# A block of linear attention and a gated feed-forward network: where one of three sums of w2 is made, and the order of steps in the key pairs, the query rounds and the reload

## The chip, the cores and the metric

The kernel runs on one core of a Trainium2 chip. The metric is the device time of one execution in microseconds (us). The kernel before takes 1144.45 us, the median of three runs (1141.81 to 1144.91).

## The reference

`x` has 2048 rows (S) and 576 columns (D). There are 32 heads of 18 columns, and the feed-forward network has 4608 columns (F). Everything is float32.

```python
phi = lambda t: where(t > 0, t + 1, exp(t)) + 1e-6
xn  = layernorm(x)
q, k, v = split(xn @ wqkv)                       # 32 heads of 18
kv  = einsum("bhsd,bhse->bhde", phi(k), v);  z = sum over s of phi(k)
o   = einsum("bhqd,bhde->bhqe", phi(q), kv) / (einsum("bhqd,bhd->bhq", phi(q), z) + 1e-6)
s   = o @ wo
g   = silu(gelu(xn @ w1 + b1) @ w2 + b2)
out = x + s * g
```

## The kernel before

**The arithmetic.** TensorE (PE) does every product in a form called fp32r. To keep float32's accuracy an operand is split in two: ScalarE (ACT) casts it to the high part, and VectorE (DVE) subtracts that from the operand to get the low part; a product is then three matmuls (high by high, high by low, low by high). Most of the large products are also cut into two by two blocks and done with seven block products instead of eight. Such products need sums and differences of blocks as operands; they are numbered 1 to 7, and 4, 5 and 6 (of w2; for other tensors others too) work on operands that are differences of blocks. GpSimd (POOL) makes most of these differences, DVE some.

**Key pairs.** The 16 row tiles of x (128 rows each) go two by two through the pairs p = 0 to 7. For a pair, x is normalised (`x_stats` on DVE and POOL, `x_norm` on ACT, line L260, tile xn), transposed on PE (`transpose_x`, L270, into the one transpose bank pt), cast (`x_hi`, xH), copied (`x_raw`, L284, scr), and subtracted (`x_lo`, xL). `x_sum` (L310, scr) makes the differences, `s_hi` and `s_lo` split them into xSH and xSL, and `x_store` writes all four to DRAM (x_dram). PE then makes k with the seven products (class Proj; four banks a, b, z and e; in the order 1, 6, 7, 5, 2, 4, 3; matmuls at L349, with ACT's copy of the first product, m1, at L361, and DVE's u1 and u2 at L357 and L367), v of both tiles plainly (class Plain, L404; ACT copies the result at L411), and adds k and v into the state (`do_state`) one pair later. Banks are handed round, so that product 7 of a pair (bank z) takes the bank that the first copy of v of the pair before has to leave. phi is `phi_exp` (ACT, L435), `phi_max` (DVE, L438) and `phi_add` (ACT, L441).

**What sets the order.** Every pair and every round has 14 steps (NSP). `add(step, fn, ...)` puts a call into the plan, and `at_step(step)` issues what stands there right behind PE's matmuls of that step. A number in these tables thus sets where an operation stands in its engine's queue. PE, DVE, ACT and POOL each keep the order in which the code is written, and each works its queue strictly in that order. The DMAs are issued by SyncE (SP).

**Query rounds.** Rounds r = 0 to 9 do the same for q, a pair of tiles in each: Proj, phi, the denominator (`den_mul` on POOL, `den_sum` on DVE, `den_div` on POOL, which writes p into pbuf), `pad` (ACT, L832), `transpose_p` (bank ptp), `p_hi` and `p_lo` (th, tl), and `Attend`, the product with kw. kw is the state times wo, made once in round 0 (`fold_wo`); its row blocks reach their place through DMAs into the tiles kr, and `split_kw` casts (L774, kw_h) and subtracts (kw_l) each.

**w2's differences.** The chunks of the feed-forward network need three differences of blocks of w2, operands 5, 6 and 4, for each of nine chunks of w2. All 27 are made ahead, in pairs 2 to 6 and rounds 2 to 7: `w2_load` reads the chunk, `w2_sum` (POOL) subtracts, `w2_hi` (ACT, L503) and `w2_lo` (DVE, L509, tile w2o) split, and the split operand is stored in DRAM. `W2_FIRST` and the loop at `2 <= r <= 7` hold the steps.

**Feed-forward chunks.** There are 9 chunks of F, and for each 2 halves of the rows; all chunks of the first half run first. A chunk has 28 steps (NS). Steps 0 to 13 are two Ups (class Up, matmuls at L1123): seven products each in the order 1, 6, 7, 5, 2, 3, 4, with banks a, b, zy, e; behind product 1 ACT copies a to mid (L1140), behind 6 DVE adds b (L1143), behind 7 it adds zy (L1146), behind 5 it writes b from e and mid (L1149), which frees e for product 3; gelu follows on ACT (g, L1131). Steps 14 to 27 are the Down products (bank pm, L1254): seven, each in two parts, in the order 1, 2, 7, 4, 5, 3, 6, and DVE adds each into macc (L1261). The operands of the Down products from gelu's result are sums on POOL (L1213 to L1222) and splits (`HOps`, h_h on ACT at L899, h_l on DVE at L902), at the steps of the table PH. Weights: class W1 loads and splits w1 (the tables P0 and P1; its differences at L918 to L924, tile w1t), class W2 loads a chunk of w2 (w2raw), makes operand 7 (`sum7`, L1176) and splits operands 1, 2, 7 and 3 at the steps of `PW2`. In the first half all split operands are also stored; the second half only loads them (W1Loaded, `W2.load`). Operands 5, 6 and 4 are loaded in the first half too (`W2_SUMS_NEXT`). At the end of the first half's last chunk, `x_swap` (L1396) reloads the four x tensors (xH, xL, xSH, xSL) from x_dram for the second half.

```python
    PW2 = {1: 3, 2: 4, 7: 5, 3: 20}
    W2_SUMS_NEXT = {4: 21, 5: 23, 6: 27}
```

Of the kernel before, what the change touches and what calls it, by code (L numbers as in the profile page):

```python
# [15 lines left out]
P = 128  # L16
# [26 lines left out]
def linear_attention_gated_ffn(ctx, tc, x, wqkv, wo, w1, b1, w2, b2, out):  # L43
# [420 lines left out]
    T_OPS = (5, 6, 4)  # L464
# [24 lines left out]
    def w2_sum(j):  # L489
        c, i = j // 3, T_OPS[j % 3]  # L490
        dst, a, b = w2_block(c, i)
        nc.gpsimd.tensor_tensor(dst, a, b, op=SUB)

    def w2_hi(j):
        if j > 8 and j % 3 == 2:
            halves = [w1p.tile([P, 3 * 2 * P], F32R, tag="wb", name=f"w2o{j}{v}") for v in "hl"]
            w2op[j] = [
                (u[:, : 2 * HD].rearrange("p (a d) -> p a d", a=2), v) for v, u in enumerate(halves)
            ]
        else:  # L500
            t = w1r.tile([P, 2, 2, HD], F32R, tag="stw", name=f"w2o{j}")
            w2op[j] = [(t[:, 0], 0), (t[:, 1], 1), (t, slice(0, 2))]
        nc.scalar.copy(w2op[j][0][0], w2_block(j // 3, T_OPS[j % 3])[0])  # L503

    def w2_lo(j):
        c, i = j // 3, T_OPS[j % 3]
        ops = w2op.pop(j)
        (h, _), (l, _) = ops[:2]
        nc.vector.tensor_tensor(l, w2_block(c, i)[0], h.bitcast(F32), op=SUB)  # L509
        w2_dram[c, i] = d = dram.tile([P, 2, 2, HD], F32, name=f"op_{c}_{i}")  # L510
        for t, v in ops[2:] or ops:
            nc.sync.dma_start(d[:, v], t.bitcast(F32))
# [53 lines left out]
    split_v(4, rest_v, DV)  # L566
    plain_v(0, 0).part(0, N14)
# [11 lines left out]
    x_hi(1, 0), x_lo(1, 0)  # L579
    x_raw(1, 0)  # L580
    x_norm(1, 1)
    s_hi(0), s_lo(0)
    load_x(2, 0)
    load_x(2, 1)
    x_store(0)
    plain_v(0, 1).part(0, N14)
    phi_exp(k_t[1], e_t[1]), phi_max(k_t[1], e_t[1])
    transpose_x(1, 1)
    x_stats(2, 0)
    x_hi(1, 1), x_lo_tmp(1), x_lo(1, 1)  # L590
    phi_add(k_t[1])
# [15 lines left out]
    W2_FIRST = {2: (0, 1), 3: (2, 3), 4: (4, 5), 5: (6, 7), 6: (8,)}  # L607

    def plan_pair(p):
# [19 lines left out]
        if p == 1:  # L629
            sums(1, (0, 0, 0, 1, 1), 2, 3, GP)  # L630
            for s in range(2):
                add(base + 8, k_sum, k_ts[0][s])
# [4 lines left out]
            add(base + 3, x_raw, 2, 0)  # L637
            add(base + 3, x_lo, 2, 0)
            add(base + 5, transpose_x, 2, 1)
            add(base + 5, x_hi, 2, 1)  # L640
            add(base + 6, x_lo, 2, 1)
            sums(2, (6, 6, 6, 6, 7), 8, 9, GP)
            add(base + 6, x_lo_tmp, 2)
            add(base + 7, wkq.split_sums, 1, DV)
            prepare(3, 0, 4, 6, 10, 11)
            prepare(3, 1, 7, 12, None, None)
# [3 lines left out]
            add(base + 5, wkq.split_sums, 0, DV)  # L650
        else:
            if p + 2 < NPAIR:
                prepare(p + 2, 0, 0, 5, 10, 11)
                prepare(p + 2, 1, 7, 11, None, None)
# [3 lines left out]
            if p + 1 < NPAIR:  # L658
                q = p + 1
                add(base + 2, transpose_x, q, 1)  # L660
                add(base + 2, x_hi, q, 1)
                add(base + 4, x_lo, q, 1)
                sums(q, (3, 3, 4, 4, 5), 7, 9, DV)
                add(base + 8, x_lo_tmp, q)
        ka, kb = k_ts[p % 2]
        ea, eb = e_t
        if p == 1:
# [3 lines left out]
            add(base + 9, k_sum, ka)  # L671
# [7 lines left out]
        add(base + 8, phi_add, kb)  # L679
        add(base + 10, k_sum, kb)  # L680
# [297 lines left out]
    for r in range(NPAIR + 2):  # L978
# [6 lines left out]
        if 2 <= r <= NPAIR:  # L985
            add(base, den_mul, r - 1, 1)
            add(base + 2, den_sum, r - 1, 0)
            add(base + 2, den_div, r - 1, 0)
            add(base + 3, den_sum, r - 1, 1)
            add(base + 3, den_div, r - 1, 1)  # L990
        if 1 <= r < NPAIR:
            add(base + 12, den_mul, r, 0)
            add(base + 4, pad, 0)
            add(base + 6, pad, 1)
# [5 lines left out]
        if 1 <= r < NPAIR:  # L1000
            a, b = q_tiles(r)
            add(base + 7, phi_exp, a, e_bufs[0])
            add(base + 7, phi_exp, b, e_bufs[1])
            add(base + 7, phi_max, a, e_bufs[0])
            add(base + 8, phi_max, b, e_bufs[1])
            add(base + 8, phi_add, a)
            add(base + (9 if r > 1 else 8), phi_add, b)
# [558 lines left out]
```

## Time and profile before

| | |
|---|---|
| median of 3 runs | 1144.45 us (1141.81 to 1144.91) |
| the profiled execution | 1145.28 us, span 1143.6 us |
| mean granted clock of TensorE | 0.992 of full speed |
| TensorE busy | 97% of the span |
| VectorE, ScalarE, GpSimd busy | 72%, 44%, 41% |
| DMA | 262 MB, 230 GB/s over the span |
| chain of work that ended last, by engine | PE 78%, DVE 7%, ACT 6%, DMA 5%, issue 2%, POOL 1% |

The profile shows one execution. "Busy" counts an engine's instructions, without the time that it waits; the chain that ended last is followed back from the last instruction, at each step to what released it. The nine chunks of the first half run from about 311 to 720 us, those of the second half from about 720 us to the end; the key pairs run up to about 150 us, and the query rounds behind them. A row of groups or of the timeline gives the start (or the line), the duration, the engine, the line, the operation, the tile written and the tiles read, the shapes, and in brackets the time for which the engine stood idle ahead of it and what ended that.

### The profile page before, as it was taken

The numbers are of one execution on the slowest core, as the hardware profiler recorded it, in microseconds if no ns is written. First come the engines' busy times: TensorE is split into PE (matmuls) and PEld (weight loads), VectorE is DVE, ScalarE is ACT, GpSimd is POOL, SyncE is SP. The second block draws the span as 40 slices with busy tenths as digits, with TensorE's granted clock in tenths as the row PEclk, the third lists the DMA queues.
The fourth block names the chain that finished last, engine by engine and source line by source line (L and its number), as shares of the span: only waits on it lengthen the run. The fifth ranks groups of instructions, "written<-read, shape, count | busy, mean of one in ns | idle before, by whom it ended". The sixth has DMA issues, their size and how long they took to land.

```text
span 1143.6 us, 18714 instructions
## 1 busy us (share of the span) xinstructions
PE 1108.3 (97%) x6924; PEld 1020.3 (89%) x6924; DVE 827.6 (72%) x1250; ACT 503.4 (44%) x913; POOL 473.8 (41%) x403
## 2 busy tenths in 40 slices
PE   8899998999999999999999999899999999999997
PEld 7799996999989989989889899798998998989987
DVE  5877755888687988878879888475574664755766
ACT  6756544544554454444544545333243242332342
POOL 5644342766552544535525543224132332241340
PEclk9999998999999999999999999899999999999999
DMA  5666535697788477495584769977666766667243
GB/s 198 251 231 263 211 108 165 232 321 262 265 307 299 170 267 260 167 333 189 215 319 172 263 242 353 358 277 227 212 203 212 231 196 222 209 206 225 83 140 117
DMA packets 91260, 262.48 MB, mean 230 GB/s; under 512 B 9822, under 2 KB 20574, under 8 KB 89120
## 3 DMA queue, kind: packets, MB, share of 16 engines
q1 hardware_dynamic: 91167, 261.27, 65.1%
q8 instruction: 55, 0.90, 0.3%
q14 instruction: 38, 0.30, 0.1%
HBM read 159.75 MB, written 100.60 MB: 228 GB/s over the span
## 4 chain that ended last, share of the span: by engine, by line
PE 78%; DVE 7%; ACT 6%; DMA 5%; issue 2%; POOL 1%; SPq 0%; DVEq 0%; ACTq 0%; POOLq 0%
PE pm L1254 32%; PE e L1123 12%; PE zy L1123 10%; PE a L1123 10%; PE b L1123 4%; DMA xSL<-x_dram 2%; PE pl L404 2%; PE pd L1371 2%; DVE w2o L509 2%; PE ps_s L872 1%; PE ps_kva L457 1%; PE e L349 1%; PE z L349 1%; DVE k L438 1%; DMA kr<-kw 1%
## 5 line engine op out<-in xcount | busy, mean ns | idle before, releaser
L1261 DVE TENSOR_TENSOR macc<-pm,macc 128x576 f32<-128x576 f32 x218 | 164.3, 754 | 56.8 <-PE pm L1254 56.2
L899 ACT CAST h_h<-g 128x512 fp32r<-128x512 f32 x204 | 120.9, 621 | 139.9 <-PE pm L1254 138.7
L902 DVE TENSOR_TENSOR h_l<-g,h_h 128x512 fp32r<-128x512 f32 x204 | 172.6, 846 | 0.0
L1222 POOL TENSOR_TENSOR mid<-g 128x512 f32<-128x512 f32 x34 | 44.0, 1295 | 197.1 <-ACT g L1131 197.1
L1123 PE MATMUL a<-xH,wa 128*128 128x512 f32 x360 | 117.1, 390 | 0.0
L1123 PEld LDWEIGHTS a<-xH,wa 128*128 128x128 f32 x360 | 67.6, 188 | 13.7
L1131 ACT ACTIVATE g<-b,b1c 128x512 f32<-128x512 f32 x36 | 24.8, 690 | 123.2 <-DVE b L1149 123.2
L1140 ACT COPY mid<-a 128x512 f32<-128x512 f32 x36 | 21.1, 585 | 108.7 <-PE a L1123 108.6
L1123 PE MATMUL e<-xSH,wb 128*128 128x512 f32 x216 | 67.8, 395 | 0.2 <-DVE b L1149 0.2
L1143 DVE TENSOR_TENSOR mid<-b,mid 128x512 f32<-128x512 f32 x36 | 24.8, 690 | 51.3 <-PE b L1123 40.1
L1219 POOL TENSOR_TENSOR g<-g 128x512 f32<-128x512 f32 x34 | 52.5, 1544 | 13.1 <-DVE h_l L902 11.8
L1216 POOL TENSOR_TENSOR g<-g 128x512 f32<-128x512 f32 x34 | 49.5, 1456 | 17.9 <-DVE h_l L902 16.6
L1123 PE MATMUL a<-xL,wa 128*128 128x512 f32 x144 | 56.2, 390 | 0.0
L1342 POOL TENSOR_TENSOR fin1l<-fin1h,fin1l 128x288 f32<-128x288 f32 x8 | 6.4, 805 | 120.0 <-DMA fin1l<-s_dram 78.1
L924 POOL TENSOR_TENSOR w1t<-w1raw 128x256 f32<-128x256 f32 x18 | 16.9, 939 | 84.8 <-DVE w L902 81.2
L1123 PEld LDWEIGHTS e<-xSH,wb 128*128 128x128 f32 x216 | 40.5, 188 | 12.7 <-DVE b L1149 4.5
L1123 PE MATMUL zy<-xSH,w 128*128 128x512 f32 x144 | 51.1, 396 | 0.0
L1123 PE MATMUL b<-xSH,w 128*128 128x512 f32 x144 | 50.9, 394 | 0.0
L1123 PE MATMUL e<-xSH,w 128*128 128x512 f32 x144 | 50.6, 392 | 0.0
L1123 PE MATMUL zy<-xH,w 128*128 128x512 f32 x144 | 50.2, 389 | 0.0
L1213 POOL TENSOR_TENSOR g<-g 128x512 f32<-128x512 f32 x34 | 47.7, 1402 | 2.7
L1156 DVE TENSOR_TENSOR e<-e,mid 128x512 f32<-128x512 f32 x36 | 25.1, 697 | 28.9 <-PE e L1123 28.9
(922 smaller groups left out, 3600.5 us busy)
## 6 DMA issues: line engine op xcount, KB each, us to landing
op<-w SPq DMA_DIRECT2D x72, 256.0 KB
w<-op SPq DMA_DIRECT2D x72, 256.0 KB
op<-w2o SPq DMA_DIRECT2D x21, 576.0 KB
w1raw<-w SPq DMA_DIRECT2D x18, 640.0 KB
w2raw<-w SPq DMA_DIRECT2D x10, 1152.0 KB
op_a<-wa SPq DMA_DIRECT2D x18, 640.0 KB
wa<-op_a SPq DMA_DIRECT2D x18, 640.0 KB
w2r<-w SPq DMA_DIRECT2D x6, 1152.0 KB
```

What stands on the lines that cost most here:

```text
L899: nc.scalar.copy(pair[0], src)
L902: eng.tensor_tensor(pair[1], src, pair[0].bitcast(F32), op=SUB)
L1123: nc.tensor.matmul(ps.rearrange("p (c j) -> p c j", c=4), st, mv, start=first and n == 0, stop=n == len(seq) - 1, skip_group_check=True,)
L1131: nc.scalar.activation(g, ps, AF.Gelu_apprx_tanh, bias=b1c[:, f : f + 1])
L1143: tt(u1_sb, B, m1_sb, op=ADD)
L1156: tt(E, E, u1_sb, op=ADD)
L1213: tt(src[5, pr], A(1, 0), A(1, 1), op=ADD)
L1216: tt(src[6, pr], src[5, pr], A(0, 0), op=SUB)
L1219: tt(src[3, pr], A(0, 1), src[6, pr], op=SUB)
L1222: tt(src[7, pr], A(0, 0), A(1, 0), op=SUB)
L1254: nc.tensor.matmul(ps[:, q, :HD], hs[p][st][:, cs], m[:, p, :], start=(n == 0 and i not in CHAIN), stop=(n == len(seq) - 1), skip_group_ch ...
L1261: nc.vector.tensor_tensor(dst, src, dst, op=ADD)
```

## The change

Four things are changed.

- *w2.* Only operands 5 and 6 (and 4 for chunk 0) are still made ahead, so 19 of the 27 sums stay in the pairs and rounds. Operand 4 of chunks 1 to 8 is made in the feed-forward chunk before: the raw chunk is loaded at step 8 instead of 22, `sum7` goes from step 2 of the chunk to step 20 of the one before, operand 2 is split at step 21, a new `sum4` makes operand 4 in operand 2's place by two subtractions on POOL at step 22, and its split follows at steps 24 and 25. Of `PW2`, operand 7 goes from step 5 to 4 and operand 3 from 20 to 6.
- *Key pairs.* In pair 1 the sums of x go ahead of phi, `x_raw` ahead of `x_lo`. In pairs 2 to 6 the norm of the next pair's second tile moves from step 11 to step 0 of the next pair, its transposes from step 2 to 3, and the sums and `x_lo` behind them; `phi_add` of the second tile goes from step 8 to 10 in all pairs.
- *Query rounds.* In rounds 0 to 2 the splits of kw, the denominators and parts of phi move to later steps.
- *The reload.* The four x tensors are reloaded in the order xSL, xSH, xL, xH at steps 12 and 13, where it was xH, xL at 13 and xSH, xSL at 15; the weight loads of that chunk move to behind them.

```diff
-    T_OPS = (5, 6, 4)
+    SUMS = [(0, 5), (0, 6), (0, 4)] + [(c, i) for c in range(1, NC) for i in (5, 6)]
...
-    x_hi(1, 0), x_lo(1, 0)
+    x_hi(1, 0)
     x_raw(1, 0)
+    x_lo(1, 0)
...
-    phi_exp(k_t[1], e_t[1]), phi_max(k_t[1], e_t[1])
+    phi_exp(k_t[1], e_t[1])
...
-    W2_FIRST = {2: (0, 1), 3: (2, 3), 4: (4, 5), 5: (6, 7), 6: (8,)}
+    W2_FIRST = {2: (0,), 3: (1, 2), 4: (3,), 5: (4, 5), 6: (6,)}
...
         if p == 1:
-            sums(1, (0, 0, 0, 1, 1), 2, 3, GP)
+            sums(1, (0, 0, 0, 1, 1), 1, 5, GP)
+            add(base, phi_max, k_ts[0][1], e_t[1])
+            add(base, phi_add, k_ts[0][1])
...
-                prepare(p + 2, 1, 7, 11, None, None)
+                add(base + 7, x_stats, p + 2, 1)
...
-                add(base + 2, transpose_x, q, 1)
-                add(base + 2, x_hi, q, 1)
-                add(base + 4, x_lo, q, 1)
-                sums(q, (3, 3, 4, 4, 5), 7, 9, DV)
-                add(base + 8, x_lo_tmp, q)
+                add(base, x_norm, q, 1)
+                add(base + 3, transpose_x, q, 1)
+                add(base + 3, x_hi, q, 1)
+                sums(q, (4, 4, 4, 5, 5), 7, 9, DV)
+                add(base + 5, x_lo, q, 1)
+                add(base + 6, x_lo_tmp, q)
...
-        add(base + 8, phi_add, kb)
+        add(base + 10, phi_add, kb)
...
+            late = 2 * (r == 2)
...
+            at = base + 2 * (r == 2)
+            add(at + 7, phi_exp, a, e_bufs[0])
...
-            add(base + 3, split_kw, 2, nc.vector)
-            add(base + 5, split_kw, 3, nc.vector)
+            add(base + 6, split_kw, 2, nc.vector)
+            add(base + 8, split_kw, 3, nc.vector)
...
-            n = 3 * (r + 1)
-            for j in range(3):
-                add(base + (0, 3, 3)[j], w2_sum, n + j)
...
+            n = 2 * r + 3
+            for j in range(2):
+                add(base + ((0, 3) if r > 2 else (4, 5))[j], w2_sum, n + j)
...
             split_kw(0, nc.vector)
-            for s in range(2):
-                den_all(0, s)
-            split_kw(1, nc.vector)
+            den_all(0, 0)
+            add(base + NSP + 2, den_all, 0, 1)
+            add(base + NSP + 3, split_kw, 1, nc.vector)
...
+        def sum4(self):
+            tt = nc.gpsimd.tensor_tensor
+            self.src[4] = self.src[2]
+            tt(self.src[4], self.src[2], self.src[7], op=SUB)
+            tt(self.src[4], self.src[4], self.src[1], op=SUB)
...
-    PW2 = {1: 3, 2: 4, 7: 5, 3: 20}
-    W2_SUMS_NEXT = {4: 21, 5: 23, 6: 27}
+    PW2 = {1: 3, 7: 4, 3: 6}
+    W2_SUMS_NEXT = {5: 23, 6: 27}
...
-            add(base + 22, w2t[step + 1].load_raw)
+            nxt = w2t[step + 1]
+            add(base + 8, nxt.load_raw)
+            add(base + 20, nxt.sum7)
+            add(base + 21, nxt.hi, 2)
+            add(base + 21, nxt.lo, 2)
+            add(base + 22, nxt.sum4)
+            add(base + 24, nxt.hi, 4)
+            add(base + 25, nxt.lo, 4)
...
-                for k, at in ((0, 13), (1, 13), (2, 15), (3, 15)):
+                for k, at in ((2, 12), (3, 12), (1, 13), (0, 13)):
                     add(base + at, x_swap, k)
```

The change takes lines out, so lines of the kernel after are 6 to 8 lower up to about L1160. The instructions of the places that the next part speaks of follow, in the order in which an engine gets them. A row is the line, the operation, the tile written and the tiles read, and the shape; numbers behind a name tell tiles of the same name apart.

ScalarE at the end of key pair 3, before: L441 is `phi_add`, L411 the copies of v, L503 the cast of w2's difference, L278 `x_hi`, L284 `x_raw`, L260 `x_norm`.

```order
L435 ACTIVATE e_161<-k_165,c_85 128x576
L441 ACTIVATE k_165<-k_165,c_86 128x576
L411 COPY v_158<-pl_1046 128x288
L411 COPY v_158<-pl_1047 128x288
L503 CAST w2o_1097<-w2r_718 128x576
L278 CAST xH<-pt_1099 128x640
L284 COPY scr<-pt_1099 128x640
L260 ACTIVATE xn_1126<-x_824,mv_1061 128x576
```

And after:

```order
L435 ACTIVATE e_161<-k_165,c_85 128x576
L411 COPY v_158<-pl_1041 128x288
L411 COPY v_158<-pl_1042 128x288
L496 CAST w2o_1090<-w2r_461 128x576
L278 CAST xH<-pt_1092 128x640
L441 ACTIVATE k_165<-k_165,c_86 128x576
L284 COPY scr<-pt_1092 128x640
L411 COPY v_159<-pl_1104 128x288
L411 COPY v_159<-pl_1105 128x288
L361 COPY mu_153<-a_1145 128x288
L260 ACTIVATE xn_1167<-x_823,mv_1056 128x576
```

The copies of the second v (v_159) and the copy of m1 of the next pair (mu) now stand ahead of the norm of the next pair's second tile.

ScalarE in query rounds 1 and 2, before: L774 is the cast of `split_kw`, L361 the copy of m1, L832 `pad`, L847 `p_hi`, L435 `phi_exp`, L441 `phi_add`.

```order
L774 CAST kw_h<-kw_2041 128x576
L774 CAST kw_h<-kr_2058 128x576
L361 COPY scr<-a_2113 128x288
L774 CAST kw_h<-kr_2071 128x576
L373 ACTIVATE scr<-a_2113,c_84 128x288
L832 COPY pbuf_2036<-pbuf_2036 128x64
L847 CAST th_2176<-ptp_2170 128x640
L774 CAST kw_h<-kr_2080 128x576
L832 COPY pbuf_2037<-pbuf_2037 128x64
L435 ACTIVATE e_2038<-scr,c_85 128x576
L435 ACTIVATE scr<-scr,c_85 128x576
L441 ACTIVATE scr<-scr,c_86 128x576 x2
```

And after:

```order
L361 COPY scr<-a_2094 128x288
L768 CAST kw_h<-kr_2046 128x576
L373 ACTIVATE scr<-a_2094,c_84 128x288
L826 COPY pbuf_2024<-pbuf_2024 128x64
L841 CAST th_2162<-ptp_2156 128x640
L826 COPY pbuf_2025<-pbuf_2025 128x64
L768 CAST kw_h<-kr_2059 128x576
L435 ACTIVATE e_2026<-scr,c_85 128x576
L435 ACTIVATE scr<-scr,c_85 128x576
L768 CAST kw_h<-kr_2068 128x576
L361 COPY scr<-a_2188 128x288
```

Each cast of a kr now stands behind the copy of m1 or the pads that it stood ahead of; the cast of the last kr stands ahead of the copy of m1 of round 2 (a_2188).

VectorE in the second Up of a chunk of the first half, before: L902 is a split (w_3__ of w2, h_l of gelu's result), L1156 and L1160 the ends of products 3 and 4 of the first Up, the other lines as above.

```order
L1156 TENSOR_TENSOR e_5119<-e_5119,mid 128x512
L902 TENSOR_TENSOR w_3__5224<-w2raw_5003,w_3__5224 128x576
L1160 TENSOR_TENSOR zy_5118<-zy_5118,mid 128x512
L1143 TENSOR_TENSOR mid<-b_5241,mid 128x512
L1146 TENSOR_TENSOR mid<-zy_5242,mid 128x512
L902 TENSOR_TENSOR h_l<-g,h_h 128x512
L1149 TENSOR_TENSOR b_5241<-e_5243,mid 128x512
```

And after:

```order
L896 TENSOR_TENSOR w_3__5166<-w2raw_4722,w_3__5166 128x576
L1151 TENSOR_TENSOR e_5080<-e_5080,mid 128x512
L1155 TENSOR_TENSOR zy_5079<-zy_5079,mid 128x512
L896 TENSOR_TENSOR w_3__5195<-w2raw_4722,w_3__5195 128x576
L1138 TENSOR_TENSOR mid<-b_5201,mid 128x512
L1141 TENSOR_TENSOR mid<-zy_5202,mid 128x512
L896 TENSOR_TENSOR h_l<-g,h_h 128x512
L1144 TENSOR_TENSOR b_5201<-e_5203,mid 128x512
```

The last of the w2 splits in this stretch (w_3__5195, operand 3) now stands between zy and mid<-b; before, it was the split of operand 7, ahead of zy.

88 lines of the change are left out of this document (39 added, 49 removed).

## The prediction

> **What bounds the kernel now.** I read the page's first part, then TensorE's waits, then stretches of the span, then rows of single places.
>
> ```profile
> span 1143.6 us, 18714 instructions
> PE 1108.3 (97%) x6924; PEld 1020.3 (89%) x6924; DVE 827.6 (72%) x1250; ACT 503.4 (44%) x913; POOL 473.8 (41%) x403
> ```
>
> TensorE is the bound nearly everywhere. The change neither adds nor removes a matmul (five transposes move by one step), so it can only remove TensorE's stalls or make new ones.
>
> TensorE's waits (who waited, for whom: us in total, times, longest):
>
> ```profile
> PE z L349 <- ACT v L411: 5.0, 5, 1.0
> PE b L1123 <- DMA xSL<-x_dram: 4.4, 1, 4.4
> PE pt L270 <- DVE scr L310: 2.8, 1, 2.8
> PE ptp L840 <- ACT pbuf L832: 2.8, 1, 2.8
> PE a L349 <- ACT scr L361: 2.7, 1, 2.7
> PE z L349 <- DVE scr L367: 2.0, 6, 0.8
> PE e L349 <- DVE rt L357: 1.1, 3, 0.6
> PE pt L270 <- ACT wkq_h L156: 1.1, 1, 1.1
> PE a L349 <- ACT v L411: 0.9, 1, 0.9
> PE e L349 <- DVE scr L357: 0.7, 3, 0.2
> ```
>
> Some 23 us of waits, nearly all at places that the diff touches. None is in the first half of the feed-forward chunks, where the change puts work in.
>
> Stretches (us; busy time of each engine; then granted clock, DMA share, GB/s): key pairs 0 and 1; query rounds 1 and 2; a chunk of the first half; the reload; the first and the second chunk of the second half.
>
> ```profile
> 0.00:55.85 55.85, 45.70 (x311) 42.75 (x312) 40.41 (x85) 37.64 (x66) 33.78 (x46) 0.97 0.61 220
> 162.45:204.37 41.92, 35.02 (x208) 31.04 (x209) 25.53 (x50) 18.23 (x37) 11.68 (x9) 0.92 0.41 136
> 446.96:492.43 45.47, 45.46 (x270) 41.10 (x269) 38.24 (x55) 21.15 (x40) 21.03 (x17) 1.00 0.64 236
> 700.00:724.00 24.00, 21.50 (x157) 20.84 (x155) 20.14 (x26) 10.81 (x15) 8.76 (x6) 1.00 1.02 403
> 719.72:772.29 52.57, 48.22 (x271) 43.13 (x269) 31.44 (x42) 19.20 (x28) 14.32 (x10) 0.94 0.85 309
> 772.29:817.39 45.10, 45.10 (x271) 41.16 (x269) 27.68 (x38) 14.51 (x24) 14.22 (x12) 1.00 0.69 219
> ```
>
> The clock is below 1.00 in the three stretches with a stall of 2.7 us or more: length times (1 - clock) is 1.7, 3.4 and 3.2 us of work lost behind the stalls. Stalls of 1 us leave it at 1.00 elsewhere.
>
> **The change, part by part.**
>
> *Key pair 1: gain 2.8 us (1.0 to 4.5).*
>
> ```profile
> 26.24 0.69 ACT L284 COPY scr<-pt 128x640 f32<-128x640 f32 x1 [1.07 <-DVE xH L294]
> 30.73 0.76 DVE L438 SCALAR_TENSOR_TENSOR k<-e,k 128x576 f32<-128x576 f32 x1
> 34.64 0.28 DVE L310 TENSOR_TENSOR scr<-scr,pt 128x128 f32<-128x128 f32 x1
> 35.06 0.77 PE L270 MATMUL pt<-ident,xn 128*128 128x128 f32 x5 [2.83 <-DVE scr L310]
> ```
>
> The transposes wait until the third x_sum has read the one transpose bank. x_raw goes ahead of x_lo and loses its 1.07 us, which reaches that chain through x_norm, s_hi and s_lo; phi_max goes behind the sums, 0.76 us more. So the sums end 1.8 us earlier, the stall falls to about 1.5 us, and the slow clock behind it (1.7 us) goes: 3 us. The 1.1 us stall before the next transposes stays or grows, since DVE and POOL now carry the same chain with TensorE pressing; their next waits are again x_sum and the v copies. I keep 2.8; the low end is all of it moving there, the high end both stalls and the clock going.
>
> *Copies of v ahead of x_norm, key pairs 2 to 5: gain 4.0 us (2 to 5); pair 7: 0.9 us (0 to 1).*
>
> ```profile
> 91.36 1.22 ACT L260 ACTIVATE xn<-x,mv 128x576 f32<-128x576 f32 x2
> 92.46 0.71 ACT L411 COPY v<-pl 128x288 f32<-128x288 f32 x2
> 92.92 0.40 PE L349 MATMUL z<-wkq_h,xSH 128*128 128x288 f32 x1 [0.98 <-ACT v L411]
> ```
>
> Product 7 of the next pair needs the bank that the first v copy frees. x_norm, 1.1 us of ACT's time, goes behind it into the next pair, where the transposes that need it come one step later, behind the state matmuls. ACT then has the copy done about 91.4, before TensorE comes at 91.9. What is late next: the k columns on DVE (x_sum and x_lo now stand ahead of them, some 1.3 us), then phi_max, s_lo; xSL then lands within half a microsecond of product 6's need. Four of the five waits of the first row go; pair 1's I leave in its term. In pair 7 phi_add no longer stands ahead of the copies.
>
> *Query rounds 1 and 2: gain 5.0 us (2 to 7).*
>
> ```profile
> 184.06 0.67 ACT L774 CAST kw_h<-kr 128x576 fp32r<-128x576 f32 x1 [4.15 <-DMA kr<-kw]
> 191.02 0.67 ACT L774 CAST kw_h<-kr 128x576 fp32r<-128x576 f32 x1 [5.99 <-DMA kr<-kw]
> ```
>
> These two casts wait for DMAs; behind them on ACT stood the copy of m1 (stall 2.7) and the pad (2.8). Both go ahead, so TensorE passes 182.2 without a stop, waits 0.7 for the pad (kr1's cast is still ahead of it), and reaches the second use of bank a in round 2 about 190.7. There the copy of m1 stands behind the cast of kr2, which cannot start before 191.0, two exponentials, and the cast of kr3: 191.0 + 2.5 + 0.4 = 193.9. A new stall of 3.3 us, which will again slow the clock, then 1.3 us until DVE's u2. Round 2 ends about 199.4 instead of 204.4. So half of what is removed returns one round later: the DMA of kr2 sets this stretch.
>
> *Rounds 3 to 7: gain 2.5 us (1 to 3.5).*
>
> ```profile
> 231.36 0.75 DVE L509 TENSOR_TENSOR w2o14l<-w2r,w2o14h 128x576 fp32r<-128x576 f32 x1
> 234.05 0.40 PE L349 MATMUL z<-wkq_h,xH 128*128 128x288 f32 x1 [0.24 <-DVE scr L367]
> ```
>
> One of three w2 splits leaves each round, 0.75 us right ahead of u1 and u2, for which z waits 0.24 and e after it as much, plus a restart in each. Rounds 3 to 7 hold ten of the twelve waits.
>
> *The reload at the half: gain 6.9 us (5 to 7.5).*
>
> ```profile
> 696.85 0.53 SPq L1396 DMA_DIRECT2D xL<-x_dram  x1
> 701.68 3.72 SPq L1396 DMA_DIRECT2D xSL<-x_dram  x1
> ```
>
> The chunk with the stall takes 52.57 against 45.10 us: 7.5 to win. The four x tensors are 7936 KB (8.1 MB); at the 403 GB/s of the row above that is 20.2 us. They start at 695.7, behind the last use of the sums, in one go and with no w2 load between them: last byte about 716, landing some 2 to 3 us later, 718.5. Need: 719.7, by xH, which is now last. I leave 0.6 for that.
>
> *The feed-forward chunks of the first half: loss 10.6 us (0 to 15).*
>
> ```profile
> 451.48 1.61 POOL L1176 TENSOR_TENSOR w2raw<-w2raw 128x576 f32<-128x576 f32 x1
> 462.15 0.58 ACT L1140 COPY mid<-a 128x512 f32<-128x512 f32 x1
> 462.34 1.30 POOL L1222 TENSOR_TENSOR mid<-g 128x512 f32<-128x512 f32 x1 [9.24 <-ACT g L1131]
> 462.77 0.69 DVE L1143 TENSOR_TENSOR mid<-b,mid 128x512 f32<-128x512 f32 x1 [1.23 <-ACT mid L1140]
> 465.48 0.69 DVE L1149 TENSOR_TENSOR b<-e,mid 128x512 f32<-128x512 f32 x1
> 466.22 0.50 PE L1123 MATMUL e<-xSH,wb 128*128 128x512 f32 x1
> 474.91 1.63 POOL L1216 TENSOR_TENSOR g<-g 128x512 f32<-128x512 f32 x1
> 475.97 1.11 DVE L902 TENSOR_TENSOR h_l<-g,h_h 128x512 fp32r<-128x512 f32 x1
> 485.70 0.68 DVE L902 TENSOR_TENSOR h_l<-g,h_h 128x512 fp32r<-128x512 f32 x1
> ```
>
> The sixth row shows no slack: product 3's e comes 0.04 us after b<-e has ended, 0.2 late already. The seventh and eighth show how DVE and POOL share: h_l runs until 477.08, 0.54 us beyond POOL's end (476.54), though it takes 0.68 alone. So an operation of DVE on two SBUF tensors and one of POOL do not overlap. First place, all 9 chunks: the split of operand 3 moves from step 20 to step 6, ahead of mid<-b. Its cast takes ACT at 462.15, so it is ready at 462.9, when POOL holds the lanes until 463.64; it ends about 464.25, and mid<-b follows 1.4 us later than now. h_l behind it no longer waits for POOL, which gives 0.7 back: e 0.73 us later, 9 x 0.73 = 6.6. Second place, 8 chunks: POOL's two sum4 operations (about 1.3 us net each, from 1.61 with waiting) follow the split of operand 2 and take the lanes when h_l of product 3 (485.70) wants them. That h_l must end by 486.6; I get 487.0, and 0.1 from a late accumulation: 8 x 0.5 = 4.0. The second place's POOL work replaces none before step 24, since W1's sums only move back there, into the idle time before the next chunk. The Trainium skill ("GPSIMD Engine Reference", section 1) says that POOL's SBUF interfaces are shared with VectorE instructions that have two SBUF inputs; the trace agrees.
>
> Removed with it: eight loads, eight POOL sums, casts and splits of the rounds (hidden but for what the rounds' terms count). The stores move along, in queues with room (DMA share 0.64).
>
> **Sum.** 2.8 + 4.0 + 0.9 + 5.0 + 2.5 + 6.9 = 22.1 won, 10.6 lost, net 11.5. The profiled execution took 1145.28 us (span 1143.6), 0.8 above the median; from the median, 1144.45 - 11.5 = 1133.
>
> **Rivals.**
>
> 1. The chunks hide the new work (ACT, at 44%, casts earlier, or POOL comes later than DVE): no loss, 1144.45 - 22 = 1122. For: DVE stands idle 1.23 us right at the first place. Against: the 0.04 us.
> 2. The other side: POOL gets the lanes ahead of every h_l, so a sum operation stands before both halves of product 3 and TensorE loses 1.1 us more per chunk there, and the first place costs 1.4: 8 x 1.6 + 9 x 1.4 = 25 lost, 1147 to 1148, slower. It decides from 1.3 us per place on (22 over 17). For: both places are tight. Against: in the rows DVE, one instruction deep ahead, gets its turn after each POOL operation.
> 3. The reload gains nothing: xH is needed 1.4 us before what was late, and lands as late as xSL did: about 6 us more, 1139.
> 4. The attention stalls only move: kr2's DMA, and pair 1's chain, return more than I count: half of 12.7 us, 1139.
> 5. The slow clock does not come from the stalls of 2.75 to 2.83 us and stays though they shrink: 1.7 us in pair 1 and 1.7 in rounds 1 and 2 of my terms fall away, 1136. For: three cases only. Against: stalls of 1 us never show it. The Trainium skill ("TensorE: Matmul & The Clock Gate", section "Why this matters for your kernels") speaks for it: no idle gaps above about 3 us, by which these gaps would be too short. The trace of before, with the clock down right behind each, does not agree.
>
> **Chances.** Forecast 0.48, its own range 1128 to 1138; rival 1 0.20, rival 2 0.08, rival 3 0.10, rival 4 0.10, rival 5 0.04. The range, 1119 to 1141, takes in rivals 1, 3, 4 and 5. Against the 0.3% (3.4 us) that a measurement can tell: faster 0.86, same 0.09 (rivals 3 and 4 at their worst, rival 2 at its mildest), slower 0.05.
>
> **What the profile after would show.** Waits of z for v: one, under 1 us, instead of five. The wait for xSL gone, clock 1.00 there, chunk about 45.7. A wait of a for scr near 180 (after the shift), of about 3 us, in round 2 instead of round 1. Chunks of the first half near 46.7 instead of 45.47, with e waiting for b L1149 by 0.9 in each, and pm for h_l. If those chunks stay at 45.5, the sharing of lanes or the order on ACT was misread; if the reload still waits, the order of landing was.

## The result and the profile after

The kernel after takes 1125.35 us, the median of 4 runs (1124.43 to 1128.4), the kernel before 1144.33 us beside it. The ratio is 0.9843 (95% interval 0.9819 to 0.9867): 19 us or 1.6% faster. The forecast was 1133 with a range from 1119 to 1141. The sign and the range hold; the gain is 7.5 us larger than forecast, which is about what the chunks did not lose (2.9 us lost, 10.6 forecast). The execution of 1128.4 us ran at a mean clock of 0.993, the other three at 0.996 or 0.997, so it lost some 3 us more to the clock (last section).

First the top of the page of the kernel after, then TensorE's waits, in the same views as before.

```profile
span 1123.3 us, 18672 instructions
PE 1103.1 (98%) x6924; PEld 1017.8 (91%) x6924; DVE 835.4 (74%) x1250; ACT 506.4 (45%) x913; POOL 483.8 (43%) x411
```

```profile
PE a L349 <- ACT scr L361: 2.6, 1, 2.6
...
PE pt L270 <- DVE scr L310: 1.6, 1, 1.6
...
PE e L1118 <- DVE b L1144: 0.9, 2, 0.7
...
PE z L349 <- DVE scr L367: 0.6, 1, 0.6
...
PE b L349 <- DVE xSL L317: 0.4, 1, 0.4
```

The five waits of z for the copies of v are gone but for 0.1 us in pair 2, as is the wait of b for xSL after the reload. What is left of the pad (ptp) is 0.6. The one long wait is that of bank a for the copy of m1, now in round 2.

The stretches (length; busy time of each engine; granted clock, DMA share, GB/s): pairs 0 and 1; rounds 1 and 2; a chunk's Ups and its Downs, first of the kernel before, then of the kernel after; chunk 0; the reload; the first chunk of the second half.

```profile
0.00:52.81 52.81, 45.30 (x311) 41.97 (x311) 36.11 (x79) 36.47 (x64) 28.80 (x42) 1.00 0.65 229
154.37:191.74 37.37, 34.05 (x210) 30.38 (x209) 26.57 (x50) 17.46 (x36) 11.41 (x9) 0.91 0.39 128
```

```profile
446.96:470.00 23.04, 23.03 (x103) 18.70 (x101) 17.85 (x26) 11.97 (x23) 10.54 (x9) 1.00 0.83 305
470.00:492.43 22.43, 22.43 (x169) 22.41 (x168) 20.39 (x29) 9.18 (x18) 10.49 (x8) 1.00 0.45 166
```

```profile
433.61:456.33 22.72, 22.72 (x103) 18.78 (x102) 18.94 (x28) 12.04 (x23) 8.87 (x8) 1.00 1.02 377
456.33:479.34 23.01, 22.91 (x169) 22.45 (x168) 22.03 (x28) 10.15 (x19) 15.46 (x11) 1.00 0.27 99
295.40:342.14 46.74, 45.91 (x270) 41.15 (x269) 39.20 (x53) 25.39 (x47) 24.45 (x19) 1.00 0.76 284
680.00:704.00 24.00, 24.00 (x166) 23.14 (x165) 20.08 (x27) 11.95 (x18) 7.98 (x6) 1.00 0.98 378
707.34:752.44 45.10, 45.10 (x271) 41.15 (x269) 31.32 (x42) 19.11 (x28) 14.38 (x10) 1.00 0.91 323
```

A chunk of the first half takes 45.73 us where it took 45.47. The two halves of a chunk went opposite ways: the Ups are 0.32 us shorter, the Downs 0.58 longer, and in the Downs VectorE is busy for 22.03 of 23.01 us.

Where the time went, from the starts of the same TensorE matmuls in both traces (us; the last two columns are what the stage gained and what was forecast for it):

| up to | before | after | shift | stage gained | forecast |
|---|---|---|---|---|---|
| product 2 in pair 2 (pairs 0, 1) | 60.39 | 57.30 | -3.1 | 3.1 | 2.8 |
| product 2 in pair 6 (pairs 2 to 5) | 134.56 | 127.27 | -7.3 | 4.2 | 4.0 |
| state in round 0 (pairs 6, 7) | 165.25 | 156.96 | -8.3 | 1.0 | 0.9 |
| first product with kw (rounds 1, 2) | 204.37 | 191.74 | -12.6 | 4.3 | 5.0 |
| chunk 0 (rounds 3 to 9) | 310.69 | 295.40 | -15.3 | 2.7 | 2.5 |
| second half (9 chunks) | 719.72 | 707.34 | -12.4 | -2.9 | -10.6 |
| second chunk of it (reload) | 772.29 | 752.44 | -19.9 | 7.5 | 6.9 |
| span | 1143.6 | 1123.3 | -20.3 | 0.4 | 0 |

The profiled spans are 20.3 apart, the medians 19.0, since the profiled execution of before was 0.95 us above its median and that of after 0.3 below.

### The profile page after: what moved, and what is told of

It reads as the page before. It is cut to its first block, busy times and chain, and to the rows that moved or that the text cites. A ratio compares the mean times of both kernels' runs of the same rounds, so it can differ in the third digit from the quotient of the medians.

```text
span 1123.3 us, 18672 instructions
## 1 busy us (share of the span) xinstructions
PE 1103.1 (98%) x6924; PEld 1017.8 (91%) x6924; DVE 835.4 (74%) x1250; ACT 506.4 (45%) x913; POOL 483.8 (43%) x411
## 4 chain that ended last, share of the span: by engine, by line
PE 81%; DVE 8%; ACT 4%; issue 3%; DMA 2%; POOL 2%; SPq 0%; DVEq 0%; POOLq 0%; ACTq 0%
PE pm L1255 32%; PE e L1118 11%; PE zy L1118 10%; PE a L1118 10%; PE b L1118 4%; PE pl L404 4%; PE ps_s L866 2%; PE pd L1372 2%; PE e L349 1%; DVE w2o L501 1%; PE z L349 1%; DMA kr<-kw 1%; DVE h_l L896 1%; PE ps_kva L457 1%; PE a L349 1%
## 5 line engine op out<-in xcount | busy, mean ns | idle before, releaser
L896 DVE TENSOR_TENSOR h_l<-mid,h_h 128x512 fp32r<-128x512 f32 x34 | 43.1, 1268 | 6.0 <-ACT h_h L893 6.0
L1126 ACT ACTIVATE g<-e,b1c 128x512 f32<-128x512 f32 x36 | 24.8, 690 | 48.8 <-DVE e L1151 48.8
```

What stands on the lines that cost most here:

```text
L896: eng.tensor_tensor(pair[1], src, pair[0].bitcast(F32), op=SUB)
L1126: nc.scalar.activation(g, ps, AF.Gelu_apprx_tanh, bias=b1c[:, f : f + 1])
```

## The experiments

Each kernel is the kernel after but for the edit shown, unless told otherwise. Times are medians; each ran beside the kernel before, whose medians were 1142.4 to 1142.7 in these runs. Beside the kernel after it was 1144.33, so a difference from after can be off by up to 2 us; the traces say how much of it belongs to the edit.

### A split one step later

```diff
-    PW2 = {1: 3, 7: 4, 3: 6}
+    PW2 = {1: 3, 7: 5, 3: 6}
```

> The kernel after, with the split of w2's operand 7 put back from step 4 to step 5 of a chunk. In the kernel after, product 3's e of the second Up waits 0.7 us for b in chunk 0 (where operand 2 is split at step 5) and not at all in chunks 1 to 8. Theory A: a split at step 5 stands ahead of zy on VectorE and holds back gelu, POOL's first sum of the second Up, and so everything that shares lanes with it; chunks 1 to 8 then look like chunk 0: the Ups take about 23.7 us instead of 22.7, each chunk 1.0 us more, 8 us in all, about 1133. Rival B: the stall went because POOL's sum7 left step 2 of these chunks; then nothing changes, 1125.

Measured: 1126.76 us (ratio 0.9865, 0.9849 to 0.9881). The Ups of chunks 1 to 8 take 22.94 us instead of 22.72: e of the second Up starts 0.09 us late in each (19.18 us into the chunk instead of 19.09), and its second matmul follows 0.33 us behind the first instead of 0.23. The chunks lose 1.7 us in all by the trace. So the split's step does matter (rival B said nothing would change), but by a quarter of the price that I set: with step 4 empty, e of the first Up ends 0.7 us earlier in the chunk (it starts at 444.43 less 433.99 instead of 444.78 less 433.61), and e starts only 0.09 us late, where in chunk 0 of after it starts 0.88 late (at 19.97).

### Leaving out POOL's new operations

`no_sum4` leaves out the two lines of sum4; `no_sums` also this one:

```diff
-            add(base + 20, nxt.sum7)
```

> The kernel after, without the two subtractions of sum4: operand 4 of chunks 1 to 8 is then the block that operand 2 is made of, all other work stays. Theory A: the Down products of chunks 0 to 7 take 23.02 us instead of 22.39 because POOL's sums delay VectorE's h_l; sum4's two operations cause the stalls ahead of product 3 and after (0.36 of the 0.63 us), sum7's at step 20 the ones ahead of product 5 (about 0.27): the Down falls to about 22.65, 8 x 0.36 = 2.9 us won, 1122.5. Rival B: it is VectorE's and ScalarE's splits moved into the Down that delay h_l: no change, 1125.

Measured: 1124.44 us (ratio 0.9844, 0.9825 to 0.9863), against 0.9843 for after: no gain. The Downs take 22.96 us, 0.05 less.

> The kernel after without sum4's two subtractions and without sum7 of chunks 1 to 8 (their operands 4 and 7 are then plain blocks); casts, splits, loads and stores all stay where they are. Theory A: it is the number of POOL's operations between its sums of gelu's result and the last h_l that costs VectorE its time; in the kernel without sum4 W1's four sums moved up behind sum7 and hit the last h_l instead. Without sum7 too, W1's sums start 1.9 us earlier, as in the kernel before, and the Downs take 22.4 to 22.5 us instead of 23.0: 8 x 0.55 = 4.4 us won, 1121. Rival B: the split of operand 2 one step later than operand 3's was is enough for the stalls: no change, 1124 to 1125.

Measured: 1120.99 us (ratio 0.9811, 0.9796 to 0.9825), 4.4 us less than after; the Downs take 22.47 us, 0.54 less. Now the Down in the three kernels: no_sum4, no_sums, and further below op2_late (the same columns as above).

```profile
455.82:478.78 22.96, 22.88 (x170) 22.46 (x168) 21.47 (x30) 9.75 (x19) 12.33 (x9) 1.00 0.28 102
```

```profile
454.46:476.93 22.47, 22.47 (x170) 22.40 (x168) 20.90 (x30) 9.76 (x19) 10.49 (x8) 1.00 0.27 106
```

```profile
455.03:477.70 22.67, 22.67 (x169) 22.42 (x168) 20.92 (x29) 9.19 (x18) 12.36 (x9) 1.00 0.25 94
```

POOL's operations in after: sum4's second one, and VectorE's h_l beside it. In no_sum4: a sum of W1 (L926) and an h_l.

```profile
472.98 1.75 POOL L1177 TENSOR_TENSOR w2raw<-w2raw 128x576 f32<-128x576 f32 x1
...
472.20 1.26 DVE L896 TENSOR_TENSOR h_l<-g,h_h 128x512 fp32r<-128x512 f32 x1
...
474.04 1.24 DVE L896 TENSOR_TENSOR h_l<-g,h_h 128x512 fp32r<-128x512 f32 x1
```

```profile
468.97 1.19 POOL L926 TENSOR_TENSOR w1raw<-w1raw,w1t 128x256 f32<-128x256 f32 x1
...
468.30 1.26 DVE L896 TENSOR_TENSOR h_l<-g,h_h 128x512 fp32r<-128x512 f32 x1
```

Without sum4, the next operations in POOL's queue, W1's sums, moved up and hit an h_l in its place, at 1.26 us instead of 0.68. Taking one operation away only let the next one do the harm; without sum7 as well, POOL is busy as long as before (10.49 us), and the loss is gone. So the price hangs on how much POOL still has to do between its sums of gelu's result and the last h_l, not on one operation. VectorE's own splits there have a part too: op2_late keeps sum7 but takes sum4 and a split out of the Down, and gets 0.35 us back, though POOL is as busy there as in no_sum4.

### w2 as before

The w2 part of the diff is undone (all 27 sums ahead, the old steps in the chunks); the rest stays as after. In round 2 three sums have to fit the later steps: sums at 4, 5, 5, casts at 10, 11, 12, splits at 11, 12, 12.

> The kernel after with w2 as before: all 27 sums made ahead in pairs and rounds (in round 2 at the later steps of the kernel after), no sum4, sum7 and the splits of operands 2, 7 and 3 in their old steps. The order in the pairs and rounds and the reload stay as after. Theory A (each term where the traces show it): the chunks of the first half give back the 3.1 us that they lost, rounds 3 to 7 lose the 2.5 us that they won, the other rounds up to 1: 1125 to 1126, no difference from after. Rival B: the move of the sums is what lets the pairs and rounds 1 and 2 run freely too: 1130 or more.

Measured: 1129.64 us (ratio 0.9888, 0.9869 to 0.9908), 4.3 us more than after. By the trace it is 7.4 us behind after when chunk 0 starts and gets 3.0 back in the chunks. Rounds 3 to 7 account for 2.8 of the 7.4, as in theory A; 1.9 are lost at the start of round 3, where z waits 2.5 us for u2 and the third split of round 2 (2.0 us on VectorE) stands right ahead of u1; the rest is spread over the head and the pairs. So A had the chunks and rounds 3 to 7 right and the rest wrong, and moving the third sum is worth some 4 us net against this layout, and 2.4 if the 1.9 are put down to where I set the third split, which was not tried elsewhere.

### The norm back ahead of the copies of v

```diff
-            add(base + 9, x_stats, 3, 1)
+            prepare(3, 1, 7, 12, None, None)
...
-                add(base + 7, x_stats, p + 2, 1)
+                prepare(p + 2, 1, 7, 11, None, None)
...
-                add(base, x_norm, q, 1)
```

> The kernel after with the norm of the next pair's second tile put back from step 0 of that pair to step 11 or 12 of the pair before; the transposes stay at step 3. Theory A: ScalarE's order made the waits of z for the copy of v; the norm's 1.1 us stand ahead of the copies again, and z waits about 1.0 us in four or five pairs: 4 to 5 us more, 1129 to 1130. Rival B: the waits went because phi_add and the sums moved; then at most 1 us more, 1125 to 1126.

Measured: 1129.7 us (ratio 0.989, 0.9872 to 0.9907), 4.35 more than after. Its row of TensorE's waits:

```profile
PE z L349 <- ACT v L411: 2.3, 5, 0.8
```

All five waits are back: 0.8 us in pair 2, and 0.3 to 0.4 in pairs 3 to 6, where they had been 1.0. But the edit moves more than the norm. Its first lines also put the statistics (`x_stats`) of a tile from step 9 of pair 1 to step 7, where VectorE now does them ahead of xSL, and pair 2 gets two waits:

```profile
52.93 0.40 PE L349 MATMUL b<-wkq_h,xSL 128*128 128x288 f32 x1 [1.12 <-DVE xSL L317]
...
54.57 0.40 PE L349 MATMUL z<-wkq_h,xSH 128*128 128x288 f32 x1 [0.83 <-ACT v L411]
```

These two and 3.4 us at half clock behind them put the trace 3.3 us behind after at product 2 of pair 2, of the 5.6 us by which this execution, the longest of the four, is behind at the end. In pairs 2 to 5, the stage of the second term, it loses 1.5 us of the 4.2 that the change won there. So ScalarE's order is shown to bring the waits back, and to be worth about a third of that stage's gain. The rest hangs on what this run left in its new place (phi_add, the sums, the transposes), which was not taken apart.

### The reload

`reload_old` puts the four x_swaps and the weight loads at their old steps; `reload_order` keeps the new steps in the old order:

```diff
-                for k, at in ((2, 12), (3, 12), (1, 13), (0, 13)):
+                for k, at in ((0, 12), (1, 12), (2, 13), (3, 13)):
```

> The kernel after with the reload as before: xH, xL at step 13, xSH, xSL at step 15, the weight loads in their old steps. Theory A: the reload's part of the result is its own 7.5 us and hangs on nothing else: the chunk after the half takes 52.6 us again with one stall above 4 us for xSL and the slow clock behind it, 1125.35 + 7.5 = 1133. Rival B: since the chunks of the first half now store and load differently (operand 4 is not loaded in them), the old reload would have come through with less loss: 1125 to 1129.

Measured: 1131.76 us (1128.56 to 1132.2; ratio 0.99, 0.9883 to 0.9917), 6.4 us more than after. The profiled execution is the fastest of these, 1128.56; its chunk after the half takes 49.98 us, with this wait:

```profile
PE b L1118 <- DMA xSL<-x_dram: 3.0, 1, 3.0
```

So the old reload by itself costs between 4.9 us (this trace) and 6.4 (the median): between A and B. Its stall is 3.0 us where the kernel before had 4.4; what took away the 1.4 us was not tested.

> The kernel after with the four x tensors reloaded at the new steps 12 and 13 but in the old order: xH, xL, xSH, xSL. Theory A: what counts is that all four start right behind the last uses with no weight load between them. xH's last use is a product later than xSL's, so all start about 1.8 us later (at 684.5 instead of 682.65), are through the queue 20.2 us later and land by about 707; xSL is needed at about 709: no stall, 1125 to 1126. Rival B: the order was needed, xSL comes last and late as before: a stall of 1 us or more ahead of b, with the slow clock if it passes 2.5 us: 1127 to 1130.

Measured: 1137.74 us (ratio 0.9958, 0.9943 to 0.9973), 12.4 more than after, and it tells nothing about landing times. My edit was faulty: at step 12 product 4 of the last Up, which reads xH, is still to come, so the load of xH stands ahead of it in the program. TensorE waits for a load that should have come after, and product 4 takes the other half's rows:

```profile
PE zy L1118 <- DMA xH<-x_dram: 10.0, 1, 10.0
```

xH and xL can only be reloaded at step 13, xSH and xSL a step earlier: the new order is what lets the reload start early. Whether the order would matter with all loads started at once was not tested.

### The casts of kr behind the copy of m1, and chunk 0

```diff
-            add(base + 6, split_kw, 2, nc.vector)
-            add(base + 8, split_kw, 3, nc.vector)
+            add(base + NSP + 2, split_kw, 2, nc.vector)
+            add(base + NSP + 3, split_kw, 3, nc.vector)
...
-            for i, at in PW2.items() if step else (*PW2.items(), (2, 5)):
+            for i, at in PW2.items() if step else (*PW2.items(), (2, 4)):
```

> The kernel after with two small moves. (1) The casts of the last two kr go to steps 2 and 3 of query round 2, behind the copy of m1 and DVE's u1 and u2. Theory A: the stall of 2.6 us at bank a in round 2 was the copy of m1 behind a cast that waits for a DMA; it goes, and with it the slow clock behind it (1.7 us): 4 us won, of which up to 1 comes back at z or ps_s. Rival B: kr2's DMA is needed itself by the product with kw in that round, and the stall moves there: under 1 us won. (2) In chunk 0 the split of operand 2 goes from step 5 to 4. Theory A: a split between e and zy costs a round trip from VectorE to ScalarE and back, 2 us; without it chunk 0 loses its wait of 0.7 us for b: its Ups take 22.7 instead of 23.7, 1.0 us won. Rival B: four splits are too many wherever they stand: no change. Both by A: 1120 to 1121.

Measured: 1120.21 us (ratio 0.9805, 0.9792 to 0.9819), 5.1 us less than after. Round 2 from 178 to 186 us in this kernel:

```profile
178.00:186.00 8.00, 7.77 (x56) 7.09 (x55) 6.73 (x12) 5.33 (x10) 3.32 (x2) 1.00 0.49 164
```

The stall and the slow clock are gone, 5.4 us by the first product with kw, of which 1.3 come back as a wait of z for the copies of s one round on. In chunk 0 the Ups fall from 23.72 to 22.69 us. Both theories A hold.

### sum7 earlier

```diff
-            add(base + 20, nxt.sum7)
+            add(base + 12, nxt.sum7)
```

> The kernel after with sum7 of the next chunk issued at step 12 instead of 20, so that POOL can do it in its idle stretch ahead of the second Up's sums; sum4 stays at step 22. Leaving sum4's operations out took only 0.05 us from a Down, since W1's sums moved up into their place. Theory A: POOL's work between its sums of gelu's result and the end of the last h_l is what VectorE loses time to; without sum7 there, the stalls ahead of product 5 (0.27 us) go, those behind sum4 (0.36) stay: 8 x 0.27 = 2.2 us won, 1123. Rival B: the splits of w2 in the Down are the cause, not POOL: no change. Rival C: sum7 then takes the lanes from the h_l that the first Down product needs: a new stall of about 0.6 us at the Down's start, 1126 to 1130.

Measured: 1143.22 us (ratio 1.0003, 0.9994 to 1.0012), 18 us more than after: worse than every theory. POOL's queue in a chunk:

```profile
467.05 1.43 POOL L1171 TENSOR_TENSOR w2raw<-w2raw 128x576 f32<-128x576 f32 x1 [4.03 <-DMA w2raw<-w]
468.44 1.87 POOL L1223 TENSOR_TENSOR mid<-g 128x512 f32<-128x512 f32 x1
```

I had seen POOL idle there and not asked whether the data had landed. sum7 waits 4 us for the raw chunk of w2, and the sums of gelu's result wait behind it in the queue; TensorE loses 1.2 to 2.2 us in each of chunks 1 to 7, and 3.8 in chunk 0, where 3.4 us at half clock follow.

### Operand 4 in the Up, operand 2 behind the last h_l, and the combinations

`op2_late`:

```diff
-            for i, at in PW2.items() if step else (*PW2.items(), (2, 5)):
+            if step:
+                add(base + 3, w2t[step].sum4)
+            for i, at in (*PW2.items(), (2, 5) if step == 0 else (4, 4)):
...
-            add(base + 21, nxt.hi, 2)
-            add(base + 21, nxt.lo, 2)
-            add(base + 22, nxt.sum4)
-            add(base + 24, nxt.hi, 4)
-            add(base + 25, nxt.lo, 4)
+            add(base + 25, nxt.hi, 2)
+            add(base + 25, nxt.lo, 2)
```

> The kernel after with sum4 and the split of operand 4 moved into the chunk's own first Up (steps 3 and 4, where POOL stands idle for 8 us) and the split of operand 2 from step 21 to 25, behind the last h_l. sum7 stays at step 20. Theory A (VectorE is the tight engine from the Down's start to the last h_l, and loses 0.6 us to each POOL operation that meets an h_l and 0.7 to each split): without the split there, the stalls ahead of product 3 (0.36 us) go, sum7's 0.27 stay: 8 x 0.36 = 2.9 won. In the Up one more split (0.7 us) stands ahead of e and zy; b for product 3's e is ready 0.9 us early now, 0.2 are left: no stall. 1122 to 1123. Rival B: sum4 and the split make the Up's b late, 0.3 to 0.7 us in 8 chunks: no gain, 1124 to 1127.

Measured: 1122.25 us (ratio 0.9822, 0.9805 to 0.9839), 3.1 less. The Downs take 22.65 to 22.67 us (its row stands above), the Ups 22.715 as before the edit: theory A with its size.

`best` joins op2_late and kw_chunk0 and moves round 2's casts and splits of w2 to step 12.

> The edits of the two runs together: the casts of the last two kr at steps 2 and 3 of round 2 and the split of operand 2 in chunk 0 at step 4 (5.1 us won over after), operand 4 made in the chunk's own first Up with the split of operand 2 at step 25 (2.9 by theory A of its own run, 0 to -2 by its rival), and in round 2 the casts and splits of w2's differences at step 12, behind the copies of s for which z then waited 1.3 us (1 us won). Together by A: 1125.35 - 9 = 1116; by the rival 1119 to 1122.

Measured: 1119.63 us (ratio 0.9803, 0.9783 to 0.9823). The third edit was a mistake; these are its wait and the cause:

```profile
PE z L349 <- DVE scr L367: 3.2, 1, 3.2
```

```profile
197.84 3.49 DVE L501 TENSOR_TENSOR w2o<-w2r,w2o 128x576 fp32r<-128x576 f32 x2 [2.06 <-POOL e L804]
```

Two splits in a row, beside POOL, stand ahead of u1 of round 3 for 3.5 us, and 3.4 us at half clock follow.

> The kernel best without its third edit: in round 2 the casts and splits of w2's differences stand at steps 10 to 12 again. There VectorE's two splits, put right ahead of u1 and u2 of round 3, had made z wait 3.2 us in place of the 1.3 us that the edit saved. Theory A: the three other edits add up, since they lie in places of their own: 1120.2 (casts of kr, chunk 0) less the 3.1 us of operand 4 and operand 2 in the Down: 1117. Rival B: the gains of the rounds and of the chunks share something (a DMA, an order on SP): 1119 to 1120.

Measured: 1117.44 us (1116.81 to 1117.69; ratio 0.9776, 0.9763 to 0.979). The edits add up, and this version is 8 us faster than the kernel after.

## Why the prediction was right, and where not

**The attention part: right in each term's size, not in all of its causes.** The table above sets the terms beside the stages: 15.3 us measured, 15.2 forecast (2.8 + 4.0 + 0.9 + 5.0 + 2.5). So close a sum is partly luck. Of the 4.2 us in pairs 2 to 5, norm_old shows 1.5 to come from the cause that the prediction gave, the norm ahead of the copies of v; the rest is not taken apart. For rounds 1 and 2 the prediction had the place and the cause of the stall that returns; the rows are ScalarE's in round 2:

```profile
182.44 0.67 ACT L768 CAST kw_h<-kr 128x576 fp32r<-128x576 f32 x1 [4.07 <-DMA kr<-kw]
...
184.92 0.39 ACT L361 COPY scr<-a 128x288 f32<-128x288 f32 x1
```

The stall is 2.6 us where 3.3 was worked out, and the slow clock behind it costs twice what was set for it (3.4 us of work, below); the 1.3 us for u2 that were expected behind it did not come. In all the term is 0.7 short. That the cast of a late kr was its cause is shown by kw_chunk0. For pair 1 the sum was right and its parts roughly: the stall is 1.6 (forecast 1.5), the clock in pairs 0 and 1 is 1.00.

**The reload: right,** 7.5 against 6.9, with the clock at 1.00 from 680 us on and the chunk after it at 45.1. The fear that xH, now last, would land 0.6 us late did not come true.

**The chunks: the step that failed.** Of the 10.6 us of loss, 2.9 came. The Downs were forecast at 0.5 us in each of 8 chunks and lost 0.58; the cause was less simple than "sum4 against h_l of product 3", as no_sum4 and no_sums show. The failure is the first place: 9 x 0.73 = 6.6 us of loss in the Ups, where chunks 1 to 8 gained 0.32 each and only chunk 0 lost. (What they gained is the lateness that the prediction had seen: e of the second Up started at 19.26 us into the chunk before and at 19.09 after, and its restart cost nearly as much again.) The working took the time at which ScalarE comes to the moved cast from the trace of before (462.15) and left out what the change removes ahead of it. Before, VectorE in the first and second Up of a chunk:

```profile
460.17 0.76 DVE L902 TENSOR_TENSOR w__5224<-w2raw,w__5224 128x576 fp32r<-128x576 f32 x1 [1.32 <-ACT w__5224 L899]
460.84 0.69 DVE L1160 TENSOR_TENSOR zy<-zy,mid 128x512 f32<-128x512 f32 x1
...
461.57 0.69 ACT L1131 ACTIVATE g<-zy,b1c 128x512 f32<-128x512 f32 x1 [1.44 <-DVE zy L1160]
```

And the same chunk after, which starts at 433.61 instead of 446.96 (13.35 less):

```profile
445.38 0.69 DVE L1155 TENSOR_TENSOR zy<-zy,mid 128x512 f32<-128x512 f32 x1
...
446.11 0.69 ACT L1126 ACTIVATE g<-zy,b1c 128x512 f32<-128x512 f32 x1
...
446.87 1.29 POOL L1223 TENSOR_TENSOR mid<-g 128x512 f32<-128x512 f32 x1 [8.08 <-ACT g L1126]
...
447.39 1.39 DVE L896 TENSOR_TENSOR w__5195<-w2raw,w__5195 128x576 fp32r<-128x576 f32 x1 [1.32 <-ACT w__5195 L893]
448.70 0.68 DVE L1138 TENSOR_TENSOR mid<-b,mid 128x512 f32<-128x512 f32 x1
...
451.09 0.70 DVE L1144 TENSOR_TENSOR b<-e,mid 128x512 f32<-128x512 f32 x1 [0.31 <-PE e L1118]
```

Before, the split of operand 7 at step 5 stood between e and zy. VectorE idled 1.32 us for its cast, which ScalarE could only do behind gelu of e, then split, and only then did zy: a round trip of 2.0 us. With operand 7 at step 4, zy follows e at once: 11.77 us into the chunk instead of 13.88, 2.1 us earlier, and gelu of zy, POOL's first sum and the moved cast with it. The moved split still meets POOL's sum, as forecast, and takes 1.39 us; but it starts early enough that b comes 1.0 us earlier in the chunk (17.48 against 18.52), not 0.7 later; by the last row VectorE even waits 0.31 us for TensorE there.

Chunk 0 is the forecast come true: there operand 2 is split at step 5, so zy stands behind a split as before, and the moved split comes on top.

```profile
308.63 0.76 DVE L896 TENSOR_TENSOR w__3675<-w2raw,w__3675 128x576 fp32r<-128x576 f32 x1 [1.31 <-ACT w__3675 L893]
309.31 0.69 DVE L1155 TENSOR_TENSOR zy<-zy,mid 128x512 f32<-128x512 f32 x1
...
315.37 0.50 PE L1118 MATMUL e<-xSH,wb 128*128 128x512 f32 x1 [0.74 <-DVE b L1144]
```

The wait is 0.74 us, the forecast 0.73 for every chunk. kw_chunk0 (operand 2 to step 4: 1.0 us back) and op7_step5 (operand 7 to step 5: 0.22 lost per chunk) show that the split's step does it. The order of VectorE's queue quoted ahead of the prediction had the fact in it, the split ahead of zy in the one and not in the other; the working read only the row that had been added.

**The rivals.** Rival 1 (no loss in the chunks, 1122) was nearer than the forecast. Of its two reasons the first held, though not because ScalarE has time to spare: it casts earlier, since the change removed a split ahead of it. The second did not hold: POOL came earlier too, not later. And the Downs did lose. Rivals 2 and 3 fell. Of rival 4 (stalls only move) one part holds: round 2, which the forecast had. Rival 5 (the slow clock is not the stalls') fell with pair 1's clock, and in kw_chunk0 the slow clock went with the stall. But the argument held against it, that stalls of 1 us never slow the clock, fails in norm_old, where two of 1.1 and 0.8 us close together did.

## What to carry to other kernels

When an operation moves ahead in an in-order queue, take its new start from the whole queue ahead of it: what the change took out there can be worth more than what it put in. A cast and split that passes between two engines is cheap before a chain that passes between the same two engines, and costs a round trip inside it. Idle time of an engine is no room for an operation whose data have not landed, and taking one operation from a crowded queue may only move the next one into its place.

## What the runs showed that I had not expected

The length of a stall alone does not tell what the clock does behind it. Behind each of the two stalls of 2.75 us of before the clock was at half for 3.4 us; behind the one stall of 2.57 us of after it stayed there for 6.8 us, from 185.15 to 191.98 us. In every trace the clock falls, and comes back, only at times that lie a multiple of 3.41 us apart. So the rows that follow are cut at these times; first the stall of round 1 before, then that of round 2 after:

```profile
182.41:185.82 3.41, 0.73 (x5) 0.73 (x6) 2.27 (x5) 0.97 (x2) 2.03 (x2) 1.00 0.80 198
185.82:189.24 3.42, 3.42 (x16) 3.31 (x15) 1.02 (x3) 0.00 (x0) 0.00 (x0) 0.50 0.78 214
189.24:192.65 3.41, 0.65 (x6) 0.41 (x5) 0.92 (x2) 1.21 (x3) 0.00 (x0) 1.00 0.23 60
```

```profile
181.74:185.15 3.41, 1.05 (x8) 0.81 (x7) 2.01 (x3) 2.71 (x5) 0.00 (x0) 1.00 0.36 100
185.15:188.56 3.41, 3.11 (x11) 2.77 (x12) 3.23 (x8) 2.60 (x5) 1.91 (x2) 0.50 0.98 406
188.56:191.98 3.42, 3.42 (x16) 3.42 (x15) 3.12 (x6) 0.24 (x1) 2.82 (x3) 0.50 1.02 411
191.98:195.39 3.41, 3.41 (x27) 3.41 (x27) 1.30 (x3) 0.25 (x1) 2.82 (x3) 1.00 0.63 234
```

In both the half clock follows a stretch in which TensorE was busy for less than half. Wherever the clock falls behind a stall in the fourteen traces, that share is 0.48 or less. Before, the slow stretch begins when TensorE works again, is busy throughout, and stays alone. After, it begins while TensorE still waits (until 185.36 us), is busy for 3.11 of 3.41 us, and a second one follows. The other traces agree but for one: where a second slow stretch followed, TensorE was busy for 0.91 or less of the first; where none did, for 0.99 or more, and once for 0.89 (reload_old, round 2).

So it counts where a stall lies against these times. Two waits of 1.12 and 0.83 us in one stretch (norm_old, from 51.65 us) brought the half clock. One of 2.46 us that was divided between two (w2_old, from 205.57 us, busy for 0.64 and 0.56 of them) did not, nor the 1.57 us of pair 1 after (0.54). A stretch that was busy for 0.45 (no_sum4, from 181.07 us) was not followed by a slow one, where one at 0.48 (sum7_12, from 326.80 us) was, so these numbers give no sharp limit. The Trainium skill ("TensorE: Matmul & The Clock Gate", section "Why this matters for your kernels") asks for no idle gaps above about 3 us; the 2.57 us here do not agree with it.
